# ConvNeXt-V2 block: the phase-2 reloads of x move from the GpSimd queue to the SP queue

## Chip, cores and metric

The kernel runs on one core of one Trainium2 chip. The metric is the device time of one execution in microseconds (us); lower is better. A kernel is run several times and the median is compared. One further execution is recorded by the hardware profiler; its trace is what the profile lines in this document come from.

## The reference

```python
# x: (1, 512, 512, 96) bf16; dw: (3, 3, 96); w1: (96, 384); w2: (384, 96); grn_gamma, grn_beta: (384,)
out = 3x3 depthwise convolution of x with dw (zero padding)
h = layernorm(out, over the 96 channels)
h = gelu_tanh(h @ w1)                                   # 384 channels a pixel
gx = sqrt((h * h).sum(over all pixels) + 1e-6)          # one number a channel
nx = gx / (gx.mean(over channels) + 1e-6)
h = grn_gamma * (h * nx) + grn_beta + h
return x + h @ w2
```

The sum over all pixels splits the work in two: `nx` is known only when the last pixel has been through the GELU, and the second matmul needs `nx`. The 384-channel tensor of all pixels (512 x 512 x 384 in bf16) does not fit on the chip.

## The kernel before

The image is worked in 128 blocks of four rows (2048 pixels). The reference's name in the code for a pixel's GELU output is `g` here.

Phase 1 (line 881 and around, up to some 950 us) goes through all blocks: convolution, layernorm, first matmul, GELU, and the sums of squares for `gx`. The normalised input of the first matmul, `yn`, is written to DRAM for every block. For 38 blocks (every third one, `is_whole`) g is written to DRAM as well; five late blocks keep g on chip (`is_held`), and three keep `yn` on chip (`KEPT`).

Between the phases the scale of each channel is computed and folded into the weights (`W2s`, lines 988 to 1025). `beta @ w2` is a constant of the output, `B2c`.

Phase 2 (line 1039) goes through the blocks in another order, `ORDER`, in which blocks with stored g and blocks whose g is recomputed alternate at about one to two. For the n-th block of that order, in program order:

- `load_rest(n + 5)` (line 283): for a block with stored g one DMA of 1536 KB into `gl` (two buffers); for a block to be recomputed three DMAs of 128 KB into a `ynT` buffer (a ring of six); nothing for the kept ones. The first is issued from `pq`, the others from `sq`.
- `load_xr(n + 5)` (line 275): one DMA of 384 KB that reads the block's x again, into `xr` (five buffers).
- `stage_xb(ORDER[n + 2])` (line 321): one addition on GpSimd, `xb` = `xr` + `B2c` in f32 (three buffers).
- `stage_mm2(n)` (line 329): 48 matmuls of 128x96 outputs in four groups of twelve; after each group DVE adds the group's PSUM bank and `xb` into `o_sb` (four buffers). After each group `pace` also issues first matmuls and GELUs for the recomputation of later blocks (`recompute`, into three buffers `gr`), so that two blocks of recomputation stand ahead.
- `stage_out` of block n-1 (line 351): one DMA of 384 KB that stores `o_sb`, from the SP queue.

`sq` is SP and `pq` is GpSimd. For the first eight blocks both are wrapped so that their instructions keep the program's order; after that the tile framework orders each engine's instructions, by their dependences. An engine executes its own in order: a DMA issue that waits holds up whatever stands behind it on that engine. The framework gives the DMAs of one queue eight completion semaphores in turn, and a DMA is issued only when the one that last used its semaphore has landed.

Before phase 2, lines 971 to 980, the loads of the first five blocks are issued from SP. The calls that the change touches are lines 1040 to 1045, and `load_xr`.

Of the kernel before, what the change touches and what calls it, by code (L numbers as in the profile page):

```python
# [57 lines left out]
def kernel(  # L58
# [125 lines left out]
    with ExitStack() as p1:  # L184
# [90 lines left out]
        def load_xr(n, pq):  # L275
            q = ORDER[n]
            r0 = q * GR
            xr = late.xr.tile([128, PXP, C], bf16, name="xr")
            pq.dma_start(out=xr[:], in_=x[0, r0:r0 + GR].rearrange("r w c -> (r w) c").rearrange(  # L279
                "(p g) c -> p g c", g=PXP))  # L280
            grp.setdefault(q, {})["xr"] = xr

        def load_rest(n, sq, pq):
            q = ORDER[n]
            v = grp.setdefault(q, {})
            if is_held(q):
                v["g"] = gs[q]
            elif is_whole(q):
                v["g"] = late.gl.tile([128, NQ, NCH, QW], bf16, name="gl")
                pq.dma_start(out=v["g"][:].rearrange("p t j w -> p (t j w)"), in_=g_dram[whole.index(q)])  # L290
            else:
                ynt = yn_ring[SLOTS[nth_made[q] % NYT]]
                if q not in KEPT:
                    for i in range(NI):
                        sq.dma_start(out=ynt[i:128:4], in_=yn_src(q)[i:C:NI])
                v["ynt"] = ynt
# [24 lines left out]
        def stage_xb(q, pq, bias):  # L321
            if q is None:
                return
            xb = late.xb.tile([128, PXP, C], f32, name="xb")
            pq.tensor_tensor(out=xb[:], in0=grp[q]["xr"][:],  # L325
                                    in1=bias[:, None, :].to_broadcast([128, PXP, C]), op=ALU.add)
            grp[q]["xb"] = xb

        def stage_mm2(n, q):
            g, xb = grp[q]["g"], grp[q]["xb"]  # L330
            GQ = QW // 128
            o_sb = late.o.tile([128, PXP, C], bf16, name="o_sb")
            for sub in range(NSUB):
                O = out_bank()
                for gl_ in range(GPS):
                    gg = sub * GPS + gl_
                    for j in range(NCH):
                        t, c = gg // GQ, gg % GQ * 128
                        pe.matmul(O[:, gl_, :], lhsT=g[:, t, j, c:c + 128], rhs=W2s[:, j, :],
                                   start=(j == 0), stop=(j == NCH - 1))  # L340
                dve.tensor_tensor(out=o_sb[:, sub * GPS:(sub + 1) * GPS, :], in0=O,
                                   in1=xb[:, sub * GPS:(sub + 1) * GPS, :], op=ALU.add)
                if n == NBLK - 1:
                    out_part(q, o_sb, sub)
                if sub == NSUB - 1 and q in nth_made:
                    used[0] += 1
                pace(n, sub)
            grp.pop(q)
            return o_sb

        def stage_out(q, o_sb):
            r0 = q * GR
            nc.sync.dma_start(
                out=out[0, r0:r0 + GR].rearrange("r w c -> (r w) c").rearrange("(p g) c -> p g c", g=PXP),
                in_=o_sb[:])

        PRE = 5
# [43 lines left out]
        n = 0  # L401
# [627 lines left out]
    with p2:  # L1029
        def out_part(q, o_sb, sub):  # L1030
            r0 = q * GR
            nc.sync.dma_start(
                out=out[0, r0:r0 + GR].rearrange("r w c -> (r w) c").rearrange(
                    "(p g) c -> p g c", g=PXP)[:, sub * GPS:(sub + 1) * GPS],
                in_=o_sb[:, sub * GPS:(sub + 1) * GPS])

        held = None
        FIRST = 8
        for n, q in enumerate(ORDER):
            sq, pq = (sp, pool) if n < FIRST else (nc.sync, nc.gpsimd)  # L1040
            if n + PRE < NBLK:
                load_rest(n + PRE, sq, pq)
                load_xr(n + PRE, pq)
            if 3 <= n + 2 < NBLK:
                stage_xb(ORDER[n + 2], pq, B2c)
            if n == NBLK - 1:
                stage_out(*held)
                held = None
            o_sb = stage_mm2(n, q)
            if held:  # L1050
                stage_out(*held)
            held = (q, o_sb)
# [30 lines left out]
```

## Time and profile before

| | us |
|---|---|
| median of 3 runs | 1457.62 (1456.41 to 1458.78) |
| profiled execution, its time | 1457.34 |
| profiled execution, its span | 1455.6 |
| GpSimd additions of line 325: count, mean | 118, 3.131 |
| GpSimd issue of an `xr` reload after the first blocks: count, median | 115, 0.553 |
| GpSimd issue of a `gl` load after the first blocks: count, mean | 36, 0.535 |
| from issue to landing, median: `xr`, `gl` | 6.7, 10.8 |

The span runs from the first instruction to the last; the time around it is launch and end. PE is TensorE, DVE VectorE, ACT ScalarE, POOL GpSimd, SP SyncE. A row of a group has its count, its busy time and mean duration in ns, and the idle time of its engine just before it with what ended it. DMA-issuing instructions on POOL have rows in the timeline, with the time that POOL spends on them, and the windows count them as busy; on SP they show as SPq. q0 is the queue of the DMAs that GpSimd issues, q1 that of those that SP issues. The DMA share is the time of all packets over the time of 16 DMA engines.

### The profile page before, as it was taken

Reading aid. Unit: us, or ns where it says so; the run is one execution under the profiler, and the core shown is the slowest. Engines: PE = TensorE matmul, PEld = TensorE weight load, DVE = VectorE, ACT = ScalarE, POOL = GpSimd, SP = SyncE. Lnnn points to the kernel's source line nnn. Section 1 sums busy time; section 2 is a strip of 40 time slices with the busy share of each in tenths; the row PEclk is TensorE's granted clock in tenths of the full one; section 3 lists DMA queues with packets and bytes.
Section 4 is the critical chain, followed back from the end, with each engine's and each line's share of the span. In section 5 each row is a group of like instructions: output and inputs, shape, how many; then the busy total and the mean of one; then the engine's idle time right before and its main releaser. Section 6 shows DMA issues by size and latency. Waiting matters only on the chain.

```text
span 1455.6 us, 55006 instructions
## 1 busy us (share of the span) xinstructions
PE 1397.3 (96%) x23465; PEld 828.7 (57%) x23465; DVE 1147.1 (79%) x2181; ACT 1392.0 (96%) x1586; POOL 1280.1 (88%) x865
## 2 busy tenths in 40 slices
PE   8989999999999999999999998799999999999998
PEld 3445545454544545454454545467777777767776
DVE  7959999999999999999999987865555555545555
ACT  6989999999999999999999999999999999989997
POOL 2588999989999998999999997569999999999998
PEclk9999999999999999999999999999999999999999
DMA  5678888888888888988888966569999999999998
GB/s 171 197 226 261 267 279 267 273 278 266 258 278 267 277 252 272 288 266 278 273 246 278 287 218 180 181 224 408 334 359 400 402 401 399 405 381 387 411 401 330
DMA packets 169212, 430.32 MB, mean 296 GB/s; under 512 B 34375, under 2 KB 84231, under 8 KB 164103
## 3 DMA queue, kind: packets, MB, share of 16 engines
q1 hardware_dynamic: 152292, 318.52, 66.3%
q0 software_dynamic: 15312, 108.14, 19.4%
q8 instruction: 183, 3.00, 0.8%
q14 instruction: 63, 0.51, 0.1%
q10 hardware_dynamic: 1362, 0.15, 0.1%
HBM read 265.70 MB, written 160.94 MB: 293 GB/s over the span
## 4 chain that ended last, share of the span: by engine, by line
PE 31%; POOL 21%; ACT 19%; DVE 13%; DMA 7%; issue 6%; SPq 3%; ACTq 0%; POOLq 0%; DVEq 0%
PE PS L36 31%; POOL xb L325 14%; ACT g L36 13%; DVE bst L36 8%; ACT y_bf L36 5%; POOL yn L36 3%; SPq L36 3%; DVE xT L36 2%; DMA yn_dram<-yn 2%; DMA ynT<-yn_dram 2%; POOL xr L279 1%; POOL ysq L36 1%; DMA rbc<-r_dram 1%; DMA xin<-in_x_dram 1%; POOL nt L36 1%
## 5 line engine op out<-in xcount | busy, mean ns | idle before, releaser
L36 ACT ACTIVATE g<-PS 128x512 bf16<-128x512 f32 (+2 forms) x1067 | 728.8, 881 | 11.6 <-PE PS L36 11.1
L36 DVE BATCH_NORM_STATS2 bst<-g 128x6 f32<-128x512 bf16 x1035 | 630.5, 674 | 46.0 <-ACT g L36 45.1
L36 ACT ACTIVATE gr<-PS 128x1536 bf16<-128x1536 f32 x348 | 485.9, 1456 | 26.1 <-PE PS L36 20.8
L36 DVE TENSOR_TENSOR o_sb<-PS,xb 128x384 bf16<-128x384 f32 x512 | 275.9, 556 | 223.2 <-PE PS L36 150.3
L36 POOL TENSOR_TENSOR yn<-y_bf,rbc 128x1536 bf16<-128x1536 bf16 x126 | 391.0, 3106 | 45.3 <-DMA rbc<-r_dram 21.2
L325 POOL TENSOR_TENSOR xb<-xr,B2c 128x1536 f32<-128x1536 bf16 x118 | 367.8, 3131 | 1.4
L36 PE MATMUL PS<-xT,Wq 64*32 64x511 bf16 (+1 forms) x9198 | 343.5, 386 | 17.2 <-ACT y_bf L36 4.7
L36 POOL TENSOR_TENSOR ysq<-y_bf 128x1536 bf16<-128x1536 bf16 x115 | 315.8, 2746 | 12.8 <-ACT y_bf L36 8.2
L36 PE MATMUL PS<-ynT,w1p 128*128 128x512 bf16 x1086 | 312.3, 380 | 13.0 <-ACT g L36 5.1
L36 PE MATMUL PS<-ynT,w1s 128*128 128x512 bf16 x984 | 267.1, 380 | 0.0
L36 PEld LDWEIGHTS <-gr 128*128 128x128 bf16 x4152 | 203.8, 98 | 54.9 <-issue 0.8
L36 PEld LDWEIGHTS <-Wq 64*32 64x32 bf16 x9216 | 108.7, 90 | 184.1 <-PE PS L36 102.8
L36 PE MATMUL PS<-W2s,gr 128*128 128x96 bf16 x4080 | 213.2, 206 | 0.3 <-DVE o_sb L36 0.2
L36 ACT ACTIVATE y_bf<-PS 128x1024 bf16<-128x1024 f32 (+1 forms) x134 | 188.8, 1414 | 12.2 <-PE PS L36 8.0
L36 DVE STREAM_TRANSPOSE xT<-xin 128x576 f32<-128x576 f32 (+1 forms) x256 | 181.7, 749 | 17.5 <-DMA xin<-in_x_dram 13.2
L36 PEld LDWEIGHTS <-w1p 128*128 128x128 bf16 x1086 | 86.7, 97 | 163.3 <-issue 113.1
L36 PEld LDWEIGHTS <-g 128*128 128x128 bf16 x2004 | 121.8, 98 | 85.3 <-issue 52.3
L36 PE MATMUL PS<-w1p,ynT 128*128 128x384 bf16 (+2 forms) x972 | 145.5, 273 | 6.2 <-ACT xT L36 2.5
L36 PE MATMUL PS<-g 128*128 128x128 bf16 x1764 | 139.9, 220 | 1.2 <-DVE PS L36 1.2
L36 PEld LDWEIGHTS <-gl 128*128 128x128 bf16 x1824 | 90.1, 98 | 41.0 <-issue 19.4
L36 PE MATMUL PS<-W2s,gl 128*128 128x96 bf16 x1824 | 97.8, 206 | 13.1 <-DVE o_sb L36 12.5
L36 PEld LDWEIGHTS <-w1s 128*128 128x128 bf16 x984 | 78.4, 98 | 39.0 <-issue 0.6
(111 smaller groups left out, 697.3 us busy)
## 6 DMA issues: line engine op xcount, KB each, us to landing
g_dram<-g SPq DMA_DIRECT2D x114, 512.0 KB
gl<-g_dram POOLq DMA_DIRECT2D x38, 1536.0 KB, 10.8
xin<-in_x_dram SPq DMA_DIRECT2D x126, 432.0 KB
yn_dram<-yn SPq DMA_DIRECT2D x512, 96.0 KB
ynT<-yn_dram SPq DMA_DIRECT2D x128, 384.0 KB
out_dram<-o_sb SPq DMA_DIRECT2D x127, 384.0 KB
xr<-in_x_dram POOLq DMA_DIRECT2D x123, 384.0 KB, 6.7
ynT<-yn_dram SPq DMA_DIRECT2D x246, 128.0 KB
```

The lines of the kernel that those rows point to most:

```text
L36: r = f(*a, **k)
L279: pq.dma_start(out=xr[:], in_=x[0, r0:r0 + GR].rearrange("r w c -> (r w) c").rearrange("(p g) c -> p g c", g=PXP))
L325: pq.tensor_tensor(out=xb[:], in0=grp[q]["xr"][:], in1=bias[:, None, :].to_broadcast([128, PXP, C]), op=ALU.add)
```

## The change

One word changes: the reload of x gets the queue `sq` and not `pq`.

```diff
@@ -1040,7 +1040,7 @@
             sq, pq = (sp, pool) if n < FIRST else (nc.sync, nc.gpsimd)
             if n + PRE < NBLK:
                 load_rest(n + PRE, sq, pq)
-                load_xr(n + PRE, pq)
+                load_xr(n + PRE, sq)
             if 3 <= n + 2 < NBLK:
                 stage_xb(ORDER[n + 2], pq, B2c)
             if n == NBLK - 1:
```

In the order of instructions, 123 DMA issues leave GpSimd and stand on SP. Phase-2 GpSimd is left with the additions `xb` and the loads `gl`, one `gl` to three additions. On SP a block's reload stands behind the `ynT` loads of the same block, where there are any, and ahead of the store of the block before the current one. The instructions of TensorE, VectorE and ScalarE and their order are the same.

## The prediction

> **What bounds the kernel now.** I read the page first, then phase 2 by windows, then one cycle of GpSimd row by row. On the page:
>
> ```profile
> PE 1397.3 (96%) x23465; PEld 828.7 (57%) x23465; DVE 1147.1 (79%) x2181; ACT 1392.0 (96%) x1586; POOL 1280.1 (88%) x865
> PE 31%; POOL 21%; ACT 19%; DVE 13%; DMA 7%; issue 6%; SPq 3%; ACTq 0%; POOLq 0%; DVEq 0%
> L325 POOL TENSOR_TENSOR xb<-xr,B2c 128x1536 f32<-128x1536 bf16 x118 | 367.8, 3131 | 1.4
> ```
>
> By busy share TensorE and ScalarE lead, but 21% of the chain that ended last is GpSimd, and the chain of waits in order of time consists, from 1049 us to 1436, mostly of the additions `xb` of line 325. The windows say why (core time, then busy time of PE, PEld, DVE, ACT, POOL, granted clock, DMA share, GB/s):
>
> ```profile
> 956.00:1045.00 89.00, 88.97 (x1323) 66.56 (x1320) 50.96 (x94) 87.57 (x64) 82.67 (x49) 1.00 0.91 337
> 985.00:1020.00 35.00, 35.00 (x525) 26.32 (x524) 19.94 (x38) 34.41 (x26) 33.96 (x22) 1.00 1.02 411
> 1085.00:1296.00 211.00, 204.17 (x3004) 151.41 (x3001) 114.48 (x215) 198.33 (x143) 205.39 (x125) 1.00 1.02 401
> 1296.00:1330.00 34.00, 31.07 (x436) 22.71 (x434) 17.11 (x32) 28.83 (x22) 30.45 (x19) 0.95 0.99 365
> 1330.00:1440.00 110.00, 107.43 (x1585) 79.57 (x1582) 61.29 (x113) 105.64 (x76) 107.02 (x66) 1.00 1.01 403
> ```
>
> Until 1045 TensorE is never idle (88.97 of 89.00); from 1085 on it loses 3% and POOL is busy 97%. The DMA share, 1.02, is the warning in this table: the 16 DMA engines have no free time either. One cycle of POOL is three blocks (one of them with stored g):
>
> ```profile
> 1155.19 0.56 POOL L279 DMA_DIRECT2D xr<-in_x_dram  x1 [0.30 <-POOL xb L325]
> 1155.74 0.53 POOL L290 DMA_DIRECT2D gl<-g_dram  x1
> 1156.29 6.21 POOL L325 TENSOR_TENSOR xb<-xr,B2c 128x1536 f32<-128x1536 bf16 x2
> 1162.44 1.10 POOL L279 DMA_DIRECT2D xr<-in_x_dram  x2
> 1163.56 3.13 POOL L325 TENSOR_TENSOR xb<-xr,B2c 128x1536 f32<-128x1536 bf16 x1
> 1166.99 0.55 POOL L279 DMA_DIRECT2D xr<-in_x_dram  x1 [0.30 <-POOL xb L325]
> ```
>
> From 1155.19 to 1166.99 is 11.80 us, and the rows fill it: 0.30 + 0.56 + 0.53 + 6.21 + 1.10 + 3.13 = 11.83. So POOL sets a pace of 11.80 per three blocks. Where TensorE set it, the twelve additions of three blocks on DVE repeat faster:
>
> ```profile
> 1000.16 1.12 DVE L36 TENSOR_TENSOR o_sb<-PS,xb 128x384 bf16<-128x384 f32 x2 [0.60 <-PE PS L36]
> ...
> 1011.47 1.12 DVE L36 TENSOR_TENSOR o_sb<-PS,xb 128x384 bf16<-128x384 f32 x2 [0.60 <-PE PS L36]
> ```
>
> That is 11.31, by the spacing of all such rows 11.30: TensorE's own pace, with ScalarE (34.41 of 35.00) just below it.
>
> **The change, part by part.** *Removed from POOL:* three issues of `xr` a cycle, 0.56 + 1.10 = 1.66 us, and the 0.30 in which an issue waits for the addition before it: 1.96 (1.66 if an addition then waits so instead). POOL's cycle becomes 11.80 - 1.96 = 9.84 (10.14), under TensorE's 11.30. POOL stops being the bound.
>
> *Added on SP:* the same three issues. Of the same shape on SP are the stores of `o_sb`, 0.34 us by the timeline; the loads of `ynT` take 0.59 (median). SP issues 6 x 0.59 + 3 x 0.34 = 4.6 us a cycle now and about 5.6 after (6.2 if a reload costs 0.55, as on POOL): half a cycle, so the issue itself costs nothing while SP has that idle half; without it, it would cost 1.0 to 1.6 a cycle.
>
> *Order on SP.* Per block: `ynT`(n+5), then `xr`(n+5), then the store of n-1. A reload waits until addition n has freed its buffer, and until the DMA eight places before it on SP has landed, since the program gives SP's DMAs eight completion semaphores in turn. Behind it wait the store, whose buffer DVE needs again four blocks later, and the next `ynT`, which TensorE needs. Addition n is finished two blocks before block n's end on the new POOL, so that wait is nothing. A reload goes out about 2 us (one store and three `ynT` loads) after the end of block n-2 and POOL may start on it four blocks after that end, 15.5 us, so it has 13 us. Stores on SP landed 4.9 to 11.3 us after issue in 1085 to 1290 by the trace's semaphore updates (median 7.9), so the reload is in time.
>
> *The DMA engines.* A cycle moves 1536 (gl) + 3 x 384 (xr) + 3 x 384 (out) + 6 x 128 (ynT) = 4608 KB, 4.72 MB; over 11.80 us that is 400 GB/s, as the window has it. The same bytes in 11.30 would need 418. In 1085 to 1296 the two queues cost alike:
>
> ```profile
> q0 software_dynamic: 6837, 49.16, 58.8%
> q1 hardware_dynamic: 12810, 34.99, 42.1%
> ```
>
> 49.16 MB / (0.588 x 211 us) = 396 GB/s and 34.99 / (0.421 x 211) = 394: moving `xr` from q0 to q1 neither saves nor costs DMA time. What then is the capacity? At least 401 to 403 (the long windows), at most a bit over 411 (985 to 1020, share also 1.02, with TensorE setting the pace and fewer stored blocks). The packets' share over 1 in all of them says that these are near the end of it. I take 407, the middle: 4.72 / 407 = 11.60 us a cycle (11.48 at 411, 11.77 at 401). So I expect the DMA engines, not TensorE, to be met next. The Trainium skill ("DMA: Bandwidth & Descriptors", Where 436 GB/s comes from) puts the ceiling at 435 GB/s: an estimate by it is 10.85 us a cycle, which would leave TensorE the bound; no window here reaches that mean.
>
> *The sum.* The steady stretches 1085 to 1296 and 1330 to 1440 are 321 us or 27.2 cycles: 27.2 x (11.80 - 11.60) = 5.4. Between them lies one POOL gap of 2.9 us before an `xr` issue that waited for nothing the profile shows; it cost DVE 4.0 and TensorE 2.9, and the clock fell (0.95 in that row). The three cycles there took 38.0 us by DVE's spacing; at 11.60 they take 34.8, since a POOL with 1.7 us of slack a cycle and three `xb` buffers rides over such a gap: 3.2. A smaller gap near 1205 made one cycle 12.45: 0.65 more. In all 9.2 us. The profiled execution took 1457.34 around its span of 1455.6, and the median of the runs is 1457.62, 0.3 above: 1457.34 - 9.2 = 1448.
>
> **The rivals.** *TensorE is met first (full gain).* If the DMA engines can do 418 GB/s, cycles go to 11.30: 27.2 x 0.50 = 13.6, the gap 38.0 - 33.9 = 4.1, the small one 0.65: 18.3, and 1439. For it: 411 was reached while DMA did not stop TensorE, and single 5 us slices show 424. Against: the packets' share was already full there.
>
> *The DMA engines are the bound already.* Then POOL only looks like it; the steady cycles gain nothing, and the gaps alone come back: 38.0 - 35.4 = 2.6 and 0.65, or 1454; none if those recur, 1457. For it: a share of 1.02 over 211 us. Against: POOL never idles on a landing, and its cycle is full without one. The Trainium skill ("DMA: Bandwidth & Descriptors", Issuing engines are not separate DMA queues) says that DMAs run on the same 16 engines whichever engine starts them and that only the sequencer's time is saved, which is this rival's reason.
>
> *SP becomes the bound (slower).* In the waits of 1085 to 1296, SP already stands for landings:
>
> ```profile
> SPq L353 <- DMA out_dram<-o_sb: 16.5, 14, 2.0
> SPq L295 <- DMA out_dram<-o_sb: 7.6, 7, 1.7
> ```
>
> Nine DMAs a cycle now, so the one eight back is 8/9 x 11.80 = 10.5 us old; with twelve it is 8/12 x 11.60 = 7.7. SP needs 12/8 = 1.5 landing times a cycle, so it decides from a mean landing of 7.9 (1.5 x 7.87 = 11.80): the median of the stores today. At 8.2 the cycle is 12.3, and 29 cycles lose 0.5 each: 1457 + 14.5 less 3 for the gaps, 1469; at 8.0, 12.0 a cycle, 1460. For it: q1's bytes rise from 1.97 to 3.15 MB a cycle. Against: gl is then alone on its queue, total bytes are the same, and a store late by one block is still in time for its buffer. The Trainium skill (same page, Queues, rings and completion order) says that each DMA engine goes round the queues packet by packet, so that gl's large packets would hold up q1's small ones; no row here shows that order.
>
> **How the numbers follow.** Forecast (a DMA floor of 403 to 411 GB/s, 1443 to 1452) 0.45; TensorE first (1439 to 1443) 0.20; nothing but the gaps (1454 to 1460) 0.15; SP the bound (1460 to 1469 and above) 0.20. What differs by under 0.2%, 2.9 us, can't be told from no change. So faster is 0.45 + 0.20 and a little of the third, 0.67; within 0.2% the rest of it, 0.13; slower 0.20. The range leaves out the end of the last case and the fastest of the second: 1440 to 1462. The forecast's own is 1443 to 1452.
>
> **What would show it.** Right: POOL busy falls from 97% to about 85% in the steady windows, DVE's wait for `xb` (44.5 us in the waits of 1085 to 1296) goes to under 10, DVE's cycle is 11.5 to 11.7, GB/s near 407 with the share still 1.02. TensorE first: a cycle of 11.30, 418 GB/s, no idle PE. DMA already the bound: 11.8 still, with POOL or TensorE now waiting for landings. SP the bound: SP's waits for landings far over the 24 us of these two rows, and DVE waiting for stores of `o_sb`. I am wrong altogether if TensorE starts to wait for `ynT`, which the reloads now stand in front of.

## The result, and the profile after

The kernel became slower. The median is 1492.72 us (1490.77 to 1501.33, six runs) against 1457.89 (1456.41 to 1460.22, six runs) beside it: 1.025 times as long, 95% interval 1.0231 to 1.0269, some 35 us. The forecast was 1448. The profiled execution after took 1501.33 around a span of 1499.6. It is the slowest of the six, so its own loss against the profiled execution before, 44.0 us, is larger than the median's. A run that took over 1.5% longer than the fastest of its kernel is left out of ratios and of what is read from them; here that is one run of e4.

The page of the kernel after: busy time by engine, the chain that ended last by engine and by line, and the group of GpSimd's additions.

```profile
PE 1410.8 (94%) x23465; PEld 836.0 (56%) x23465; DVE 1147.8 (77%) x2181; ACT 1393.0 (93%) x1586; POOL 1217.0 (81%) x742
PE 28%; DMA 26%; ACT 25%; DVE 10%; POOL 4%; issue 4%; SPq 3%; ACTq 0%; DVEq 0%; POOLq 0%
PE PS L36 28%; DMA out_dram<-o_sb 18%; ACT g L36 17%; ACT y_bf L36 6%; DVE bst L36 6%; DMA ynT<-yn_dram 3%; POOL yn L36 2%; DMA yn_dram<-yn 2%; SPq L36 2%; DMA xin<-in_x_dram 2%; DVE xT L36 1%; DMA rbc<-r_dram 1%; DVE o_sb L36 1%; ACT xT L36 1%; POOL nt L36 1%
L325 POOL TENSOR_TENSOR xb<-xr,B2c 128x1536 f32<-128x1536 bf16 x118 | 369.2, 3128 | 86.5 <-DMA xr<-in_x_dram 50.6
```

POOL's share of the chain falls from 21% to 4%, as meant. In its place stand DMAs, 7% before and 26% now, and 18% of the chain are the stores of `o_sb` (78.5% of the chain of 1085 to 1296 alone, in which there was no DMA before). The additions themselves take 3.128 us as before (3.131), but 86.5 us of idle time now stand in front of them, more than half of it spent on reloads that have not landed. Before it was 1.4.

The windows after, with the columns of the prediction's table:

```profile
985.00:1020.00 35.00, 35.00 (x528) 26.42 (x527) 19.93 (x38) 34.35 (x26) 30.21 (x12) 1.00 0.99 373
1085.00:1296.00 211.00, 188.32 (x2679) 138.74 (x2677) 102.56 (x191) 177.63 (x128) 158.32 (x64) 0.97 0.98 358
1330.00:1440.00 110.00, 97.30 (x1405) 71.98 (x1403) 54.38 (x101) 93.69 (x68) 83.53 (x34) 0.98 0.99 364
```

From 985 to 1020 TensorE is never idle, as before. From 1085 on it loses 22.7 of 211 us where it lost 6.8, and every engine is less busy, POOL too (75% for 97%). The DMA engines move 358 GB/s and not 401, while their share is still 0.98. The granted clock is 0.97 in this stretch. So no engine that computes is full any more, and the share of the DMA engines does not show that they do less.

The waits of 1085 to 1296 after (time in all, times, longest), engines first:

```profile
DVE o_sb L36 <- DMA out_dram<-o_sb: 35.3, 12, 4.5
ACT gr L36 <- PE PS L36: 31.7, 22, 4.7
POOL xb L325 <- DMA xr<-in_x_dram: 31.1, 12, 3.7
PE PS L36 <- DVE o_sb L36: 22.7, 13, 3.4
```

and SP's queue:

```profile
SPq L353 <- DMA xr<-in_x_dram: 48.8, 13, 6.1
SPq L295 <- DMA out_dram<-o_sb: 29.9, 32, 6.0
SPq L353 <- DVE o_sb L36: 8.5, 12, 1.2
SPq L295 <- DMA xr<-in_x_dram: 7.9, 13, 2.1
SPq L279 <- DMA ynT<-yn_dram: 4.7, 4, 2.1
```

Before, the same stretch had these two rows of SP beside those of the prediction, and this one of VectorE:

```profile
SPq L353 <- DVE o_sb L36: 85.2, 41, 4.4
SPq L353 <- DMA ynT<-yn_dram: 3.9, 7, 1.3
DVE o_sb L36 <- POOL xb L325: 44.5, 45, 2.1
```

SP stands for landings 48.8 + 29.9 + 7.9 + 4.7 = 91.3 us of 211; before, all rows of this kind came to 28.0. A store (L353) does not need the reload that its row names: it stands for it because that reload used the same completion semaphore. By the trace's issues and landings SP never has more than eight DMAs under way; from 1085 to 1290 it has all eight 42% of the time, 14% before. Before, the store stood mostly for its own data (DVE, 85.2 us; now 8.5). Behind SP, VectorE now stands 35.3 us for stores, because its next `o_sb` buffer is not free, and POOL 31.1 for reloads. VectorE's wait for `xb` (44.5 before) is gone.

One cycle of SP shows it (start, duration, how many):

```profile
1176.03 0.53 SPq L279 DMA_DIRECT2D xr<-in_x_dram  x1
1176.65 0.38 SPq L353 DMA_DIRECT2D out_dram<-o_sb  x1
1177.12 0.38 SPq L279 DMA_DIRECT2D xr<-in_x_dram  x1
1177.59 1.03 SPq L353 DMA_DIRECT2D out_dram<-o_sb  x1
1178.71 1.82 SPq L295 DMA_DIRECT2D ynT<-yn_dram  x3
1180.63 0.54 SPq L279 DMA_DIRECT2D xr<-in_x_dram  x1
1185.45 0.35 SPq L353 DMA_DIRECT2D out_dram<-o_sb  x1
```

GpSimd in the same cycle:

```profile
1175.81 0.57 POOL L290 DMA_DIRECT2D gl<-g_dram  x1
1176.40 3.13 POOL L325 TENSOR_TENSOR xb<-xr,B2c 128x1536 f32<-128x1536 bf16 x1
1180.10 3.12 POOL L325 TENSOR_TENSOR xb<-xr,B2c 128x1536 f32<-128x1536 bf16 x1 [0.57 <-DVE o_sb L36]
1185.54 3.12 POOL L325 TENSOR_TENSOR xb<-xr,B2c 128x1536 f32<-128x1536 bf16 x1 [2.32 <-DMA xr<-in_x_dram]
```

and VectorE:

```profile
1186.40 1.02 DVE L36 TENSOR_TENSOR o_sb<-PS,xb 128x384 bf16<-128x384 f32 x2 [2.45 <-DMA out_dram<-o_sb]
```

SP issues eight DMAs within 5.2 us and then nothing for 4.3 us. The large load `gl` went out just before them, at 1175.81, and by the trace's semaphore updates it lands at 1185.21. The first of the eight, a reload issued at 1176.03, lands at 1185.38, the others until 1190.0. Between 1180.4 and 1185.4 one DMA of 384 KB lands on SP's queue; in the 4.8 us after `gl` has landed, some 2 MB do. The packets of the trace say why: from 1178 to 1183 GpSimd's queue gets through 111 packets, of 12288 bytes, and SP's through 102, of 3072 and 4096 bytes. The turns are equal, so the bytes are four to one. So the window of eight fills while `gl` loads, SP stands still until `gl` is through, the store waits behind it, and then POOL stands 2.32 us for x and VectorE 2.45 for a buffer.

The mean cycle of three blocks, by the spacing of the blocks' last additions on VectorE, is 13.39 us from 1085 to 1290, against 11.80 before. From the 34th block to the last it is 13.02, against 11.80. Those 94 blocks are 31.3 cycles, and 31.3 x (13.02 - 11.80) = 38.2. The profiled execution after also came 5.4 us later to its first addition of phase 2 (960.5 for 955.1), by delays in phase 1, where the two kernels have the same instructions. The two make up 43.6 of the 44.0 that the profiled executions differ by, so the change itself costs some 38 in this one. From the 9th block to the 34th the cycle is 11.27 before and 11.26 after: there TensorE still leads.

### The profile page after: what moved, and what is told of

Read it like the earlier page. It is cut to its first block, busy times and chain, and to the rows that moved or that the text cites. A ratio compares the mean times of both kernels' runs of the same rounds, so it can differ in the third digit from the quotient of the medians.

```text
span 1499.6 us, 55129 instructions
## 1 busy us (share of the span) xinstructions
PE 1410.8 (94%) x23465; PEld 836.0 (56%) x23465; DVE 1147.8 (77%) x2181; ACT 1393.0 (93%) x1586; POOL 1217.0 (81%) x742
## 4 chain that ended last, share of the span: by engine, by line
PE 28%; DMA 26%; ACT 25%; DVE 10%; POOL 4%; issue 4%; SPq 3%; ACTq 0%; DVEq 0%; POOLq 0%
PE PS L36 28%; DMA out_dram<-o_sb 18%; ACT g L36 17%; ACT y_bf L36 6%; DVE bst L36 6%; DMA ynT<-yn_dram 3%; POOL yn L36 2%; DMA yn_dram<-yn 2%; SPq L36 2%; DMA xin<-in_x_dram 2%; DVE xT L36 1%; DMA rbc<-r_dram 1%; DVE o_sb L36 1%; ACT xT L36 1%; POOL nt L36 1%
## 5 line engine op out<-in xcount | busy, mean ns | idle before, releaser
L325 POOL TENSOR_TENSOR xb<-xr,B2c 128x1536 f32<-128x1536 bf16 x118 | 369.2, 3128 | 86.5 <-DMA xr<-in_x_dram 50.6
L36 PE MATMUL PS<-ynT,w1s 128*128 128x512 bf16 x984 | 271.9, 386 | 0.0
L36 PE MATMUL PS<-W2s,gl 128*128 128x96 bf16 x1824 | 101.3, 210 | 42.1 <-DVE o_sb L36 41.9
L36 PEld LDWEIGHTS <-gl 128*128 128x128 bf16 x1824 | 93.5, 100 | 70.9 <-issue 50.8
```

The source lines that it names most:

```text
L36: r = f(*a, **k)
L325: pq.tensor_tensor(out=xb[:], in0=grp[q]["xr"][:], in1=bias[:, None, :].to_broadcast([128, PXP, C]), op=ALU.add)
```

## The experiments

Two theories stood at the start. *W*, the window: SP issues in order with eight completion semaphores, and twelve DMAs a cycle in place of nine, which land late while `gl` loads, do not fit. *R*, the rate: with x on q1 the DMA engines themselves move less, 358 GB/s for 401, and SP's waits only follow. The queues' rows of 1085 to 1296 after (packets, MB, share of 16 engines' time) left R open:

```profile
q1 hardware_dynamic: 18295, 49.97, 62.7%
q0 software_dynamic: 2304, 25.17, 34.8%
```

25.17 MB / (0.348 x 211 us) is 343 GB/s, and 49.97 / (0.627 x 211) 378; before, the two queues had 396 and 394. Packets of both take longer than they did, those of 12288 bytes 571 ns in the mean (492 before; the median is 460 in both). In each experiment the time before was measured again beside it: its median is 1458.25 for e1 to e4, 1460.89 for e5 to e8, 1461.19 for e9 to e11 and 1461.53 for e12. A loss in us is counted from the one that belongs to it.

**Fewer DMAs on SP, on the kernel after (e1) and before (e2).** In place of three DMAs of 128 KB onto every fourth partition, one of 384 KB onto 96 adjacent partitions; `w1p` is in that order of rows. A cycle then has eight DMAs on SP after the change (12 without the edit), five before it (9).

```diff
-                    for i in range(NI):
-                        sq.dma_start(out=ynt[i:128:4], in_=yn_src(q)[i:C:NI])
+                    sq.dma_start(out=ynt[:C], in_=yn_src(q))
...
-            cm_unit(grp[q]["g"], grp[q]["ynt"], t, w1p if q in KEPT else w1s)
+            cm_unit(grp[q]["g"], grp[q]["ynt"], t, w1p)
```

> The changed kernel (reloads of x on SP), but the recomputed blocks' yn is loaded by one DMA of 384 KB and not by three of 128 KB; the same bytes, 8 DMAs on SP per three blocks and not 12. Theory W (window): SP can have eight DMAs under way, and with twelve per cycle landing after some 8.9 us it can't keep up (12/8 x 8.7 = 13.0 a cycle, measured 12.9). Then 8/8 x landing is under 11.5, SP keeps up, the cycle falls to 11.4 to 11.7, over 400 GB/s, and the time to 1440 to 1455. Theory R (rate): with x on SP's queue the DMA engines only move 358 GB/s at a full share; then nothing changes, a cycle of 12.9 and 1485 to 1497.

> The kernel before (reloads of x on GpSimd) with the one-DMA load of yn: the control of the run before it. Both theories: GpSimd still sets 11.8 a cycle, 1454 to 1459. If this alone is much faster or slower, the one-DMA load does something else than to lower the count.

Measured: e1 1505.75, ratio 1.0325 (1.027 to 1.0379); e2, the control, 1492.51, 1.0228 (1.0209 to 1.0247). The control decides: the same load on the kernel before costs 34 us, with x on GpSimd. Its packets of 4096 bytes take 192 ns (165 before), its stores land after 13.8 us (median; 7.9 before), its cycle is 13.13 and its rate 370 GB/s from 1085 to 1296. The edit brings a slowdown of its own, and e1 says nothing of the count. Its time is above both of its expectations, and the control came out far above what was expected of it. Between the two the move of the reloads still costs 13 us, although SP has only eight DMAs a cycle there: they land after 12.5 us in the mean, and 8/8 x 12.5 is not far below the cycle of 13.12.

**More DMAs on SP, no bytes, x still on GpSimd (e3, e5).** On the kernel before, two (e3) or one (e5) DMAs of 256 bytes a block are added on SP: fifteen or twelve a cycle for nine. In the expectation of e5, C takes the count for the whole cause, and Q the queue on which x's bytes travel.

```diff
             grp.setdefault(q, {})["xr"] = xr
+            if pq is not sp or n >= PRE:
+                for _ in range(2):      # e5: range(1)
+                    tiny = late.tiny.tile([16, 8], bf16, name="tiny")
+                    nc.sync.dma_start(out=tiny[:], in_=x[0, r0, :16, :8])
```

> The kernel before, and two more DMAs of 256 bytes per block on SP (16 partitions of 16 bytes of x into scratch tiles that nothing reads): 15 DMAs on SP per three blocks and not 9, no bytes to speak of. Theory W: SP needs 15/8 landings a cycle, with landings of 7.0 to 7.9 a cycle of 13.1 to 14.8, and 1490 to 1530. Theory R: the rate of the DMA engines is what it was, 11.8 a cycle and 1456 to 1461.

> The kernel before with one more DMA of 256 bytes per block on SP: 12 DMAs on SP per three blocks, as in the changed kernel, but x still comes from GpSimd and the extra ones carry no bytes to speak of. Theory C (the count alone): as slow as the changed kernel, a cycle of 12.6 to 13.2 and 1485 to 1500. Theory Q (the count matters only with landings as long as x's bytes make them, some 8.9 us and not 7): SP needs 12/8 x 7 = 10.5 a cycle and GpSimd still sets 11.8: 1456 to 1466.

Measured: e3 1527.82, 1.0475 (1.0452 to 1.0498); e5 1479.31, 1.0116 (1.0088 to 1.0144). The window of e3 and, in the next fence, its main new wait:

```profile
1085.00:1296.00 211.00, 185.25 (x2545) 135.82 (x2542) 97.16 (x181) 170.19 (x122) 178.03 (x109) 0.94 0.97 346
```

```profile
DVE o_sb L36 <- DMA out_dram<-o_sb: 36.1, 13, 5.0
```

The window of e5, and a row of its SP queue:

```profile
1085.00:1296.00 211.00, 196.59 (x2831) 145.47 (x2829) 108.53 (x202) 187.61 (x135) 196.71 (x120) 0.98 1.00 379
```

```profile
SPq L299 <- DMA out_dram<-o_sb: 60.8, 32, 5.0
```

e3 leaves the reloads on GpSimd and adds next to no bytes, and yet it falls to 346 GB/s with a share of 0.97, its packets of 12288 bytes take 581 ns, and VectorE stands for stores as it does after the change. So R falls as the cause: the rate drops, and the packets stretch, when SP issues late. W expected this time of e3. e5 has the count of the changed kernel and none of its bytes. Its added DMAs land after 7.4 us in the mean, hardly sooner than the others (7.8 and 8.7), so each holds its place as long as they do. It loses 18 us of the 35, half, and came between its two expectations: the count alone is one part, and something goes with where x travels. Its cycle is 12.58 from 1085 to 1290 and 11.75 after 1324, so at twelve the queue stands at the edge.

**Shorter bursts of `gl` (e4, e9).** On the kernel after, `gl` is cut into four DMAs issued together (e4), or into two halves of 768 KB, the second issued one block later (e9).

```diff
# e4
-                pq.dma_start(out=v["g"][:].rearrange("p t j w -> p (t j w)"), in_=g_dram[whole.index(q)])
+                for t in range(NQ):
+                    pq.dma_start(out=v["g"][:, t].rearrange("p j w -> p (j w)"),
+                                 in_=g_dram[whole.index(q)][:, t * NCH * QW:(t + 1) * NCH * QW])
# e9
+                    def load_half(pq, h=h, g=v["g"], k=whole.index(q)):
+                        pq.dma_start(out=g[:, 2 * h:2 * h + 2].rearrange("p t j w -> p (t j w)"),
+                                     in_=g_dram[k][:, h * half:h * half + half])
...
+            while second:          # at the head of the next block
+                second.pop()(pq)
```

> The changed kernel with each load of stored g issued as four DMAs of 384 KB, so that its packets are 3 KB and not 12 KB. Theory W with packet-by-packet sharing: while g is loaded SP's queue gets half of the engines and not a fifth, its landings shorten to 8 us or less, the cycle falls to 11.8 to 12.3, time 1456 to 1475. Theory W with the count alone deciding, or theory R: 12.9 a cycle and 1485 to 1497.

> The changed kernel with each load of stored g issued in two halves of 768 KB, the second one block later. If the burst of g on the other queue is what holds SP's DMAs up: landings of 8 us or less and 1465 to 1478 (four quarters issued together gave 1484.5). If it is the number of DMAs on SP: 1482 to 1495, like the changed kernel.

Measured: e4 1481.64 (three runs, 1471.19 to 1487.39), 1.0145 (1.0092 to 1.0199), by the ratio some 15 us better than the change alone and short of the burst's expectation; the packets of `gl` came out at 6144 bytes, not the 3072 that were meant. e9 1474.16, 1.0088 (1.0055 to 1.0121): 13 us of the 35 are left, as the theory of the burst expected. The window of e9:

```profile
1085.00:1296.00 211.00, 199.46 (x2929) 148.05 (x2928) 112.84 (x211) 193.94 (x140) 182.15 (x88) 1.00 1.01 386
```

With the same bytes, and the same twelve DMAs on SP, the reloads land after 7.5 us (median from the end of the issue; 8.9 with `gl` whole), the stores after 7.6 (9.2), and the cycle is 12.09. How `gl` is loaded makes more than half of the loss. Two things change at once in e9: the burst is spread over time, and its packets have 6144 bytes where they had 12288. Where GpSimd's queue moves 100 KB or more in half a microsecond, it moves 4.9 times the bytes of SP's after the change and 2.3 times in e9. e4 has packets of the same size and no spread in time, and its interval overlaps that of e9; what the spread adds to the smaller packets is not shown.

**The store's own place (e7, e8).** A fifth `o_sb` buffer (e7; `Wq` goes to a pool that ends with phase 1, which makes the room), or the reload issued after the store of the block before and not ahead of it (e8).

```diff
# e7
-                late.o = p2.enter_context(tc.tile_pool(name="o", side="right", bufs=4))
+                late.o = p2.enter_context(tc.tile_pool(name="o", side="right", bufs=5))
# e8
                 load_rest(n + PRE, sq, pq)
-                load_xr(n + PRE, sq)
...
             held = (q, o_sb)
+            if n + PRE < NBLK:
+                load_xr(n + PRE, sq)
```

> The changed kernel with five buffers for o_sb and not four (room made by freeing the convolution weights after phase 1). Theory W (SP's eight DMAs under way, at 12/8 landings a cycle): VectorE waits less for stores but x's reloads are late all the same, the cycle stays at 12.7 to 13.1, 1487 to 1497. If the stores' latency against four buffers is what binds: a cycle of 12.2 or less and 1475 or less.

> The changed kernel with a block's reload of x issued after the store of the block before the current one, not ahead of it: the same 12 DMAs per three blocks in another order. Theory W: the count and the landings are the same, 12.7 to 13.1 a cycle and 1485 to 1500. If the store's place behind a reload that waits is the cause: 1470 or less.

Measured: e7 1483.53, 1.0163 (1.0121 to 1.0205), between its two expectations; e8 1504.04, 1.0281 (1.0249 to 1.0313), a little above the upper one. The waits of e7 in 1085 to 1296, in its slowest run (1494.40):

```profile
POOL xb L326 <- DMA xr<-in_x_dram: 47.0, 16, 5.2
DVE o_sb L36 <- DMA out_dram<-o_sb: 25.9, 13, 4.5
```

A buffer more takes 12 us off (22.6 are left), and VectorE's wait for stores falls from 35.3 to 25.9, but POOL then stands 47.0 us for reloads and not 31.1. That is what a full queue does: with one consumer relieved, the next late DMA is felt. And changing places within a block gains nothing (e8 is no better than the change, if anything a little worse): not the order of two DMAs counts, but that SP stands for landings at all.

**The gain that was expected, without SP (e6, e11).** What is it worth to relieve POOL with every DMA left on its queue? In e6, on the kernel before, GpSimd adds only the first half of x to `B2c`, and the second half of each output block uses the first half's sums. In e11 VectorE does the additions of one block in six, in two steps (`B2c`, then x), with a sixth `xr` buffer, for which `Wq` makes the room as in e7; it computes the whole output.

```diff
# e6
-            pq.tensor_tensor(out=xb[:], in0=grp[q]["xr"][:],
+            pq.tensor_tensor(out=xb[:, :2 * GPS], in0=grp[q]["xr"][:, :2 * GPS],
...
-                                   in1=xb[:, sub * GPS:(sub + 1) * GPS, :], op=ALU.add)
+                                   in1=xb[:, sub % 2 * GPS:(sub % 2 + 1) * GPS, :], op=ALU.add)
# e11
+            return ORDER.index(q) >= 8 and ORDER.index(q) % 6 == 4    # by_dve(q)
...
+                if by_dve(q):
+                    dve.tensor_tensor(out=xb[:, here, :], in0=O,
+                                      in1=B2c[:, None, :].to_broadcast([128, GPS, C]), op=ALU.add)
+                    dve.tensor_tensor(out=o_sb[:, here, :], in0=xb[:, here, :],
+                                      in1=grp[q]["xr"][:, here, :], op=ALU.add)
```

> The kernel before, but GpSimd adds B2c only to the first half of each block's x, and the second half of the output uses that first half's sums (output not the reference's): GpSimd's cycle falls from 11.8 to about 7.2 while every DMA stays on its queue. It measures what freeing GpSimd is worth with nothing given to SP. If the DMA engines end it at 403 to 411 GB/s (the forecast's step): a cycle of 11.5 to 11.7, 1445 to 1452. If TensorE ends it: 11.3 and 1438 to 1443. If the DMA engines were the bound already: 11.8 and 1454 to 1458.

> The kernel before with every DMA on its queue; for one block of six VectorE adds B2c and x itself (two additions per group and not one) and GpSimd's addition is left out, with a sixth buffer for x. GpSimd's cycle falls from 11.8 to about 10.2, VectorE has 5 us idle a cycle and gets about 1 to 1.2 more. If freeing GpSimd without touching SP is what pays: 1450 to 1456, as with the halved addition. If the longer additions hold TensorE's PSUM banks, or nothing is gained: 1458 to 1466.

Measured: e6 1455.2 (ten runs, 1449.08 to 1463.72), 0.9959 (0.994 to 0.9979); e11 1454.86 (twelve runs, 1449.6 to 1465.05), 0.996 (0.9936 to 0.9985). The window of e6, then that of e11:

```profile
1085.00:1296.00 211.00, 206.58 (x3053) 153.91 (x3052) 117.69 (x220) 202.25 (x146) 129.52 (x129) 1.00 1.02 409
```

```profile
1085.00:1296.00 211.00, 207.55 (x3060) 154.50 (x3057) 140.10 (x255) 202.32 (x146) 180.91 (x120) 1.00 1.02 408
```

Both mean cycles are 11.61 us, at 409 and 408 GB/s, although POOL is busy only 61% in e6 and 86% in e11. The prediction had a floor of the DMA engines at 11.60 and 407. The mean agrees, but it does not come from such a floor. The chains of 1085 to 1296, of e6 and then of e11:

```profile
by line: PE PS L36 56.2%; DMA out_dram<-o_sb 39.0%; DVE o_sb L36 3.4%; POOL xb L325 0.8%; issue 0.5%; DVEq L36 0.1%; SPq L353 0.0%
by line: PE PS L36 80.6%; DVE o_sb L36 10.7%; DVE xb L36 7.4%; issue 1.5%; DVEq L36 0.0%
```

In e6, 34 of the 53 spacings of three blocks are at most 11.35, which is TensorE's own pace; the mean is longer because VectorE stands eight times for a store that has not landed (10.3 us in all). In e11 there is no DMA in the chain: TensorE leads, and all of its 3.4 idle us are spent on VectorE, whose additions take longer there. And later e11 goes on for 45 us at a rate above that floor:

```profile
1356.00:1401.00 45.00, 44.54 (x656) 33.11 (x655) 30.02 (x55) 43.69 (x32) 38.64 (x26) 1.00 1.02 419
```

The whole gain is 6 us, counted from the 1460.89 and 1461.19 of the kernel before beside these runs. The 1455.2 of e6 is above what the DMA floor had given it (1445 to 1452), 3 us of it because the kernel before read 3 us more there too. e11 is faster than both kernels of this study; the sixth buffer without the additions was not tried.

**One reload in three on SP (e10).** On the kernel after, only the blocks with stored g have their reload issued from SP: ten DMAs a cycle there, and POOL is left with some 11.2 us a cycle.

```diff
-                load_xr(n + PRE, sq)
+                load_xr(n + PRE, sq if is_whole(ORDER[n + PRE]) else pq)
```

> Reloads of x from SP only for the blocks with stored g, one of three, the others from GpSimd: 10 DMAs on SP per three blocks, GpSimd's cycle 11.8 - 0.55 = 11.25 or a little less. If each DMA more on SP costs its share (9: 1458, 12 with x: 1493): 1464 to 1472. If SP bears one more and GpSimd is free of the bound: 1452 to 1457, as with the halved addition.

Measured: 1474.52, 1.0098 (1.0065 to 1.013), above both expectations; the kernel before read 3 us more beside it than beside the change, and less these it stands at the end of the first. SP's queue and the engines show a wait that the prediction had put at nothing:

```profile
SPq L279 <- POOL xb L325: 47.2, 16, 3.3
```

```profile
DVE o_sb L36 <- POOL xb L325: 35.2, 26, 2.5
POOL xb L325 <- DMA xr<-in_x_dram: 21.9, 17, 2.4
```

Here POOL is again late with its additions, and the reload on SP must wait for the addition that frees its buffer: SP stands 47.2 us for POOL (in the kernel after there is no such row in this stretch), with the stores and `ynT` loads behind it. On POOL's own queue the same wait was harmless, since the addition stood ahead of it there anyway. A middle way between two queues is not a middle price.

**Halves and five buffers together (e12).** The edits of e9 and e7 on the kernel after.

> The changed kernel with both of the edits that helped: stored g in two halves a block apart (alone 1474.2) and five buffers for o_sb (alone 1483.5). If the two take away different parts of the loss: about 1465. If both mend the same lateness of SP's queue: 1470 to 1476. If SP is then no bound at all and the DMA engines end the cycle at 11.6 as with the halved addition: 1450 to 1456, and the change would pay after all.

Measured: 1460.0 (ten runs), 0.9989 (0.9969 to 1.0009): as fast as the kernel before, 5 us below the 1465 expected of two separate parts, and short of the gain of e6. Its window, and its wait for stores:

```profile
1085.00:1296.00 211.00, 206.42 (x3037) 154.01 (x3036) 117.44 (x218) 200.93 (x145) 186.26 (x91) 0.99 1.02 396
```

```profile
DVE o_sb L36 <- DMA out_dram<-o_sb: 6.7, 5, 3.3
```

Of the 35 us the two edits recover 22 and 12 alone, and all together. All reloads are still on SP, and its eight places are full 43% of the time, as after the change (42%). What the change lost is therefore lost by late landings and by buffers too few to ride over them, and not by the reloads' being on SP as such.

## Why the prediction was wrong, point by point

**POOL.** Right that it set the pace by its own work, 97% busy: relieving it takes VectorE's wait for `xb` away (44.5 us; 1.8 in e6, no such row in e11). The gain there is 6 us for 9.2. Of the parts, the steady cycles gave what they should, 27.2 x (11.80 - 11.61) = 5.2 for 5.4; what became of the 3.9 for the two gaps was not followed.

**The DMA floor.** Right in the number, 11.61 for 11.60, and by luck. A ceiling at 407 GB/s is not what the runs meet: e11 keeps 419 for 45 us. The mean of e6 comes from cycles at 11.30 and some with a late store, that of e11 from TensorE and VectorE. "The packets' share over 1" says little of the limit, as the last section shows. That x costs nearly the same DMA time on both queues holds: 246 ns for a packet of 6144 bytes on GpSimd's queue, 128 ns for one of 3072 on SP's. But it means twice as many packets for the same x, which counts where queues take turns.

**SP's issue cost.** Right that the time of issuing itself is nothing: the eight DMAs of the cycle shown go out in 5.2 us, and SP then stands idle.

**Order on SP: the step that failed.** "so it has 13 us" was set against the landing of one store, with a median of 7.9. Three things were left out of it. First, the 13 us count from an issue that "goes out about 2 us (one store and three `ynT` loads) after the end of block n-2", and that presumes that SP is free to issue it: with the eight-place rule, which the same paragraph names, it goes out when an older DMA lands. Second, the rule binds every DMA on SP, the store above all, whose delay costs VectorE a buffer after four blocks. Third, landings are no constant. They cluster: 9.4 us for the reload issued behind `gl` in the cycle shown, and several within a few hundred ns once `gl` is through.

**The rival "SP becomes the bound".** It had the mechanism and the sign, a chance of 0.20, and too small a price: 1460 to 1469 "and above" for a measured 1492.72. It judged by the stores' median of 7.9, which stood just at the point where it decides (7.87). Over all DMAs on SP, counted from the start of the issue, the mean in the kernel before was already 8.17, which is beyond it: 12/8 x 8.17 = 12.26 a cycle. e5, with that count alone, ran 12.58 in the same stretch and lost 18 us; the rival's price for a landing of 8.2 was a cycle of 12.3 and 12 us, so this part was of the right size and somewhat low. What it lacked is the second half. After the change the mean is only 8.29, and 12/8 x 8.29 = 12.4, yet the cycle is 13.39: twelve landings in series over eight places are a lower bound, which holds if all eight are always in flight. Here SP issues in bursts, stands still behind `gl`, and then waits for consumers that have stopped. e9, with `gl` in halves, comes down to 12.09, e12 to the kernel before.

**A large load on the other queue.** The Trainium skill ("DMA: Bandwidth & Descriptors", Queues, rings and completion order) says that each DMA engine goes round its queues packet by packet. The trace agrees: the 111 and 102 packets from 1178 to 1183 are equal turns. The prediction set it aside with "no row here shows that order". It follows from the packets that SP's queue, with the small ones, lands one reload in 5 us while `gl` loads, and 2 MB in the next 5; with `gl` in halves and at half the packet size, SP's landings are 1.3 to 1.6 us shorter. It was a reason to give this rival more than 0.20, since the change moves 384 KB a block from the queue of large packets to that of small ones.

**What would have shown it.** The sign named for this rival, "SP's waits for landings far over the 24 us of these two rows, and DVE waiting for stores", is what the profile shows: 91.3 and 35.3. TensorE does not wait much for `ynT`, so the last of the warnings did not come about.

**Open.** Why packets take longer when the queues run short (460 ns in the median, but 571 for 492 in the mean) was not settled; e3 shows only that it comes without any reload on SP. A smaller count on SP with the same spread of partitions was not tried. And the loss parts into count (18 us, e5) and the loads of `gl` (22 recovered, e9) only roughly: the two sum to more than the 35, since a shorter landing also makes the count matter less. How much of the 22 is the size of the packets and how much their spread in time stays open.

## What to carry to other kernels

Before moving DMAs to another engine's queue, count what is in flight there: DMAs per cycle times mean landing (from the start of the issue, over all DMAs of the queue) against the number of completion semaphores, and treat the result as a lower bound if a large load in large packets on another queue makes the landings come in clusters. An engine with idle issue time is not a queue with free places. To relieve an engine that is full, try moving its computing before its DMAs: here one block in six on VectorE, with one buffer more, gained 6 us (0.996, 0.9936 to 0.9985) where moving the reloads lost 35.

## What the hardware showed that was not expected

The DMA share is no measure of how near the DMA engines are to their limit. It lay between 0.97 and 1.02 in the window of 1085 to 1296 at every rate from 346 (e3) to 409 GB/s (e6): packets stretch to fill the time, some of them far more than others (the median of those of 12288 bytes is 460 ns before and after). The GB/s of a stretch against the best that the same mix has reached tells more.

A DMA of 256 bytes costs its place, not its bytes: one more a block, 768 bytes in a cycle of 4.72 MB, cost 18 us in all, and two cost 70.

One load onto 96 adjacent partitions, in place of three onto every fourth, slowed the DMAs of both queues: packets of 4096 bytes from 165 to 192 ns, those of 6144 from 246 to 269, 401 to 370 GB/s, 34 us (e2), at the same bytes. The cause was not followed.
